# Two row tiles of x turned on TensorE, the rest by the crossbar, at the head of a linear-attention kernel

## The chip, the cores and the metric

The kernel runs on one core of one Trainium2 chip. The metric is the device time of one execution in microseconds (us). The profiled execution also has a span, from its first to its last instruction, which is about 1.7 us shorter than the time. All points in time in this text ("at 7.49 us") count from the start of that span. TensorE is PE in the profile, its weight loads PEld, VectorE DVE, ScalarE ACT, GpSimd POOL, SyncE SP. The crossbar is the DMA route that transposes a matrix while it loads it. A load lands when its last byte is there and the engines that wait for it are told. PSUM is the memory that TensorE writes to.

## The reference

```python
B, S, D = 1, 2048, 640                    # H = 32 heads of 20
qkv = (x @ wqkv) ...                      # q, k, v: [B, H, S, 20]
phi = lambda t: jnp.where(t > 0, t + 1, jnp.exp(t)) + 1e-6
pq, pk = phi(q), phi(k)
kv  = einsum("bhsd,bhse->bhde", pk, v);  z = einsum("bhsd->bhd", pk)
num = einsum("bhqd,bhde->bhqe", pq, kv); den = einsum("bhqd,bhd->bhq", pq, z)[..., None] + 1e-6
return (num / den) ... @ wo
```

The kernel never makes v. It makes phi(k) for all 16 row tiles of 128 rows first (the "K phase"), then P = x^T phi(k) (the "P phase"), and works on from there. The K phase needs x with the model dimension on the partitions (`xT`), the P phase needs x in its natural layout (`xn`).

## The kernel before

Each engine has its own list of instructions; a small planner adds a semaphore wait wherever one reads what another wrote.

```python
XCH = [(0, 256), (256, 512), (512, 1024), (1024, 1536), (1536, 2048)]
def load_xT():                                  # SP queue: crossbar transposes straight from HBM
    for i, (a, b) in enumerate(XCH):
        P.add("sp", lambda e, a=a, b=b: e.dma_start_transpose(
            xT[...][:, :, a:b], x[0, a:b, :]), writes=[("xT", i)], dma=True)

def load_wk():                                  # ACT queue: wk in two halves of its columns
    w_cols(wk, 0, HALF, D, ("wk", 0), "act")
    w_cols(wk, HALF, D, D, ("wk", 1), "act")
    ...                                         # (load of the ACT table)

def warm(n):                                    # fillers: matmuls of zeros that nobody reads
    for _ in range(n):
        P.add("pe", lambda e: e.matmul(bank(7), zero[:, 0:128], zero[:, :], start=True, stop=True), ...)

def k_tile(st):
    for h in range(2):                          # five matmuls 128x128 by 128x320 for each half of wk
        ...  P.add("pe", mm, reads=xT_keys(128 * st, 128 * st + 128) + [("wk", h)], ...)
    ...                                         # exp on ACT, two steps of phi on DVE

load_wk(); load_xT(); pool_const(); load_rest() # load_rest: wq, xn (natural x), wv, wo on the SP queue
permute_wq()
warm(16)
for st in range(NT):
    k_tile(st)
...                                             # P phase, q tiles, and the rest: untouched by the change
```

Of the kernel before, what the change touches and what calls it, by code (L numbers as in the profile page):

```python
# [7 lines left out]
ALU = mybir.AluOpType  # L8
BF16 = mybir.dt.bfloat16
# [73 lines left out]
def bass_standalone__linear_attn_block__prompt_kernel(nc, x, wqkv, wo, out):  # L83
    B, S, D = x.shape
    assert (B, S, D) == (1, 2048, 640)
    H, DH = 32, 20
    NC_ = D // 128
    NT = S // 128
    HALF = D // 2
# [5 lines left out]
    with contextlib.ExitStack() as ctx:  # L95
        es = ctx.enter_context

        def sb(name, cols, dt=BF16):
            return es(nc.sbuf_tensor(name, [128, cols], dt))

        xT = sb("xT", NC_ * S)
        xn = sb("xn", NT * D)
        wk = sb("wk", NC_ * D)
# [4 lines left out]
        pk = sb("pk", NT * D)  # L108
# [13 lines left out]
        ones = sb("ones", 8, F32)  # L122
        eps = sb("eps", 8, F32)
        zero = sb("zero", BK)
        lb = [sb(f"lb{j}", BK, F32) for j in range(2)]
        rd = [sb(f"rd{j}", BK) for j in range(2)]
        osb = [sb(f"osb{j}", D) for j in range(4)]
# [3 lines left out]
        P = Plan(nc, es)  # L131

        def bank(b, n=BK, off=0, parts=128):
            return ps[0:parts, BK * b + off:BK * b + off + n]

        def two_banks(b, n=HALF, parts=128):
            return ps[0:parts, BK * b:BK * b + 2 * BK].rearrange(
                "p (g j) -> p g j", j=BK)[:, :, 0:n]

        def fold(ap, j=HALF):  # L140
            return ap.rearrange("p (g j) -> p g j", j=j)


        def pool_const():
            P.add("dve", lambda e: e.memset(zero[:, :], 0.0), writes=["zero"])
            P.add("dve", lambda e: e.memset(ones[:, :], 1.0), writes=["ones"])
            P.add("dve", lambda e: e.memset(eps[:, :], 1e-6), writes=["eps"])  # L147
            P.add("pool", lambda e: e.memset(wv[:, NC_ * D:], 0.0), writes=["wvpad"])
            P.add("pool", lambda e: e.memset(hm[:, :], 1.0), writes=["hm"])
            P.add("pool", lambda e: e.memset(bm[:, :], 1.0), writes=["bm"])  # L150
            for t, w, name in ((hm, 4, "hm"), (bm, DH, "bm")):
                n = t.shape[1] // w
                for lo in (True, False):
                    P.add("pool", lambda e, t=t, w=w, n=n, lo=lo: e.affine_select(
                        out=t[:, :].rearrange("p (a b) -> p a b", b=w),
                        in_=t[:, :].rearrange("p (a b) -> p a b", b=w),
                        pattern=[[-w if lo else w, n], [0, w]],
                        base=0 if lo else w - 1,
                        channel_multiplier=1 if lo else -1,
                        compare_op=ALU.is_ge, fill=0.0), reads=[name], writes=[name])  # L160

        XCH = [(0, 256), (256, 512), (512, 1024), (1024, 1536), (1536, 2048)]

        def xch_of(row):
            return next(i for i, (a, b) in enumerate(XCH) if a <= row < b)

        def load_xT():
            for i, (a, b) in enumerate(XCH):
                P.add("sp", lambda e, a=a, b=b: e.dma_start_transpose(
                    xT[:, :].rearrange("p (c s) -> p c s", s=S)[:, :, a:b], x[0, a:b, :]),  # L170
                    writes=[("xT", i)], dma=True)

        def xT_keys(a, b):
            return [("xT", i) for i, (p, q) in enumerate(XCH) if p < b and a < q]

        def w_cols(dst, lo, hi, col, key, eng):
            P.add(eng, lambda e: e.dma_start(
                dst[:, 0:NC_ * D].rearrange("p (c n) -> p c n", n=D)[:, :, lo:hi],
                wqkv[:, col + lo:col + hi].rearrange("(c p) n -> p c n", p=128)),
                writes=[key], dma=True)  # L180

        def load_wk():
            w_cols(wk, 0, HALF, D, ("wk", 0), "act")
            w_cols(wk, HALF, D, D, ("wk", 1), "act")
            tl = mybir.InstLoadActFuncSet(
                name=nc.get_next_instruction_name(),
                act_func_set_id=ACT_TABLE_SET_LN_EXP, ins=[], outs=[])
            P.add("act", lambda e: e.add_instruction(tl), writes=["table"])

        def load_rest():  # L190
            w_cols(wqn, 0, D, 0, "wqn", "sp")
            for q in range(4):
                P.add("sp", lambda e, q=q: e.dma_start(
                    xn[:, 4 * q * D:4 * (q + 1) * D].rearrange("p (t n) -> p t n", n=D),
                    x[0, 512 * q:512 * (q + 1), :].rearrange("(t p) n -> p t n", p=128)),
                    writes=[("xn", q)], dma=True)
            w_cols(wv, 0, D, 2 * D, "wv", "sp")
            P.add("sp", lambda e: e.dma_start(
                wog[0:GW, 0:5 * D].rearrange("p (g n) -> p g n", n=D),
                wo[0:5 * GW, :].rearrange("(g p) n -> p g n", p=GW)),  # L200
                writes=["wog"], dma=True)
            P.add("sp", lambda e: e.dma_start(
                wog[0:gsz[5], 5 * D:6 * D], wo[5 * GW:D, :]), writes=["wog5"], dma=True)

        def permute_wq():

            for d in range(NC_):
                P.add("pool", lambda e, d=d: e.tensor_copy(  # L208
                    wqp[:, d * D:(d + 1) * D].rearrange("p (c h j) -> p c h j", c=NC_, j=4),
                    wqn[:, d * D:(d + 1) * D].rearrange("p (h c j) -> p c h j", c=NC_, j=4)),  # L210
                    reads=["wqn"], writes=[("wqp", d)])


        def warm(n):
            for _ in range(n):
                P.add("pe", lambda e: e.matmul(  # L216
                    bank(7), zero[:, 0:128], zero[:, :], start=True, stop=True),
                    reads=["zero"], writes=[("bank", 7)])

        def k_tile(st):  # L220
            b = 2 * (st % 4)
            for h in range(2):
                def mm(e, h=h):
                    for c in range(NC_):
                        r = e.matmul(  # L225
                            bank(b + h, HALF),
                            xT[:, c * S + 128 * st:c * S + 128 * st + 128],
                            wk[:, c * D + HALF * h:c * D + HALF * (h + 1)],
                            start=(c == 0), stop=(c == NC_ - 1))
                    return r  # L230
                P.add("pe", mm, reads=xT_keys(128 * st, 128 * st + 128) + [("wk", h)],
                      writes=[("bank", b + h)])
            banks = [("bank", b), ("bank", b + 1)]
            t = ek[st % 3]
            P.add("act", lambda e: e.activation(fold(t[:, :]), two_banks(b), ACTF.Exp),  # L235
                  reads=banks + ["table"], writes=[("ek", st % 3)])
            P.add("dve", lambda e: e.tensor_scalar(  # L237
                t[:, :], t[:, :], 1.0, 1e-6, ALU.min, ALU.add),
                reads=[("ek", st % 3)], writes=[("ek", st % 3)])
            P.add("dve", lambda e: e.scalar_tensor_tensor(  # L240
                fold(pk[:, st * D:(st + 1) * D]), two_banks(b), 0.0, fold(t[:, :]),
                ALU.max, ALU.add),
                reads=banks + [("ek", st % 3)], writes=[("pk", st)])

        def p_step(h, st):

            def mm(e):
                for d in range(NC_):
                    r = e.matmul(  # L249
                        bank(d, HALF), xn[:, st * D + 128 * d:st * D + 128 * d + 128],  # L250
                        pk[:, st * D + HALF * h:st * D + HALF * (h + 1)],
                        start=(st == 0), stop=(st == NT - 1))
                return r
            P.add("pe", mm, reads=[("xn", st // 4), ("pk", st)],
                  writes=[("bank", d) for d in range(NC_)])

        def p_out(h):
# [171 lines left out]
                reads=[("osb", j, 0), ("osb", j, 1)], writes=[("out", st)], dma=True)  # L429


        load_wk()
        load_xT()
        pool_const()
        load_rest()
        permute_wq()
        warm(16)
        for st in range(NT):
            k_tile(st)
        zst = z_steps()  # L440
        qs = [(s, c) for s in range(NSB) for c in range(NC_)]
        qi = [0]
# [5 lines left out]
        for h in range(2):  # L448
            for st in range(NT):
                p_step(h, st)  # L450
                if zst and st % 2 == 1:
                    zst.pop(0)()
                if st == 7:
                    next_q(5 + qi[0] % 3)
            p_out(h)
            next_q(5 + qi[0] % 3)
            next_q(5 + qi[0] % 3)
# [91 lines left out]
```

## Time and profile before

| | before |
|---|---|
| time, median of 4 runs (range) | 111.82 us (111.79 to 111.96) |
| span of the profiled run | 110.1 us |
| TensorE busy | 101.5 us, 92% |
| first K matmul | 7.49 us |
| first P matmul | 30.05 us |

The page's first part says that TensorE is the busy engine.

```profile
PE 101.5 (92%) x662; PEld 64.0 (58%) x668; DVE 66.9 (61%) x132; ACT 41.9 (38%) x73; POOL 5.9 (5%) x16
```

That figure counts 16 filler matmuls as work. What holds the start is in the chain of waits of the first 33 us (start us, length us, what). Each step was released by the one above it.

```profile
...
0.81 6.55 DMA xT<-in_x_dram
7.36 0.14 issue
7.49 20.55 PE ps L225 x150
...
30.05 3.02 PE ps L249 x21
```

The first crossbar transpose is issued at 0.81 us and takes 6.55 us to land. Then K (L225) runs, and then P (L249). TensorE's own list of waits says the same (who waited for whom: us in total, times, longest).

```profile
...
PE ps L225 <- DMA xT<-in_x_dram: 1.1, 1, 1.1
PE ps L249 <- DVE pk L240: 0.7, 1, 0.7
```

K has one wait, at its start. Behind it matmuls follow each other every 136 ns, 1.36 us for a row tile of ten, and K's 160 matmuls follow one another without a hole. P's wait of 0.7 us is for phi of a late K tile, and moves with K.

Landing times of each load, worked out from the trace as its issue plus its time to landing: wk's first half 4.71 us, its second half 7.35; crossbar pieces 7.36 (rows 0-255), 8.18 (256-511), 11.11 (512-1023), 14.47, 16.83.

### The profile page before, as it was taken

To read this page: it belongs to the slowest core of one execution; us is meant where nothing else is said; L and a number is where in the kernel's file an instruction comes from. 1 tells how busy PE (TensorE), PEld (TensorE's weight loads), DVE (VectorE), ACT (ScalarE), POOL (GpSimd) and SP (SyncE) were. 2 spreads that over 40 slices of the span, in tenths; PEclk is the share of its full clock that TensorE was granted. 3 is DMA by queue.
4 is the path that set the end of the run, shared out by engine and by line. 5 is a ranking of instruction groups with operands and counts; after the bars stand their busy time and mean duration, and the time that the engine had idled before them with its cause. 6 is when DMAs were issued, how large, how long until landed. Compare 5 with 4: busy or idle time off the path is not lost.

```text
span 110.1 us, 1693 instructions
## 1 busy us (share of the span) xinstructions
PE 101.5 (92%) x662; PEld 64.0 (58%) x668; DVE 66.9 (61%) x132; ACT 41.9 (38%) x73; POOL 5.9 (5%) x16
## 2 busy tenths in 40 slices
PE   5969999999799999999999999993999799999990
PEld 2327777777477674676757745431446377777760
DVE  1004888998899899701137664969849837333331
ACT  3104555555500206202043379872575173333330
POOL 7100000750000000000000000000000000000000
PEclk9999999999999999999999999999999999999999
DMA  1999999999980000000000000082720032433333
GB/s 40 270 295 220 224 211 298 378 363 364 258 163 22 0 0 3 0 0 0 6 0 3 0 0 0 18 216 70 206 92 0 0 119 92 152 119 119 119 120 118
DMA packets 19497, 12.88 MB, mean 117 GB/s; under 512 B 10914, under 2 KB 19490, under 8 KB 19490
## 3 DMA queue, kind: packets, MB, share of 16 engines
q1 hardware_dynamic: 18178, 11.96, 39.4%
q10 hardware_dynamic: 1312, 0.82, 2.7%
q8 instruction: 5, 0.08, 0.3%
q14 instruction: 2, 0.02, 0.0%
HBM read 6.72 MB, written 3.44 MB: 92 GB/s over the span
## 4 chain that ended last, share of the span: by engine, by line
PE 70%; DVE 15%; DMA 6%; ACT 5%; issue 1%
PE ps L225 19%; PE ps L416 17%; PE ps L249 15%; PE ps L275 12%; DMA xT<-in_x_dram 6%; DVE pq L288 4%; PE ps L391 4%; DVE za L294 4%; ACT eq L283 2%; DVE eq L285 2%; DVE pq L407 2%; PE ps L344 1%; ACT lb L398 1%; PE ps L365 1%; ACT rd L400 1%
## 5 line engine op out<-in xcount | busy, mean ns | idle before, releaser
L275 PE MATMUL ps<-xT,wqp 128*128 128x512 bf16 x95 | 23.0, 379 | 2.0 <-DVE pq L288 1.8
L249 PE MATMUL ps<-pk,xn 128*128 128x320 bf16 x160 | 22.4, 299 | 0.8 <-DVE pk L240 0.7
L225 PE MATMUL ps<-wk,xT 128*128 128x320 bf16 x160 | 21.9, 299 | 1.1 <-DMA xT<-in_x_dram 1.1
L416 PE MATMUL ps<-w2p,pq 128*128 128x320 bf16 x160 | 22.2, 299 | 0.3 <-DVE pq L288 0.3
L249 PEld LDWEIGHTS ps<-pk,xn 128*128 128x128 bf16 x160 | 15.5, 98 | 7.9 <-DVE pk L240 1.0
L225 PEld LDWEIGHTS ps<-wk,xT 128*128 128x128 bf16 x160 | 15.6, 98 | 7.5 <-issue 1.5
L283 ACT ACTIVATE eq<-ps 128x512 bf16<-128x512 f32 x20 | 11.9, 595 | 21.2 <-PE ps L275 20.7
L416 PEld LDWEIGHTS ps<-w2p,pq 128*128 128x128 bf16 x160 | 15.6, 98 | 7.0 <-DVE pq L288 0.6
L235 ACT ACTIVATE ek<-ps 128x640 bf16<-128x640 f32 x16 | 11.3, 704 | 15.7 <-PE ps L225 15.7
L275 PEld LDWEIGHTS ps<-xT,wqp 128*128 128x128 bf16 x100 | 9.6, 98 | 12.2 <-DVE pq L288 2.2
L288 DVE SCALAR_TENSOR_TENSOR pq<-ps,eq 128x512 bf16<-128x512 f32 x20 | 13.8, 692 | 0.7
L285 DVE TENSOR_SCALAR eq<-eq 128x512 bf16<-128x512 bf16 x20 | 5.8, 290 | 12.8 <-ACT eq L283 12.6
L240 DVE SCALAR_TENSOR_TENSOR pk<-ps,ek 128x640 bf16<-128x640 f32 x16 | 13.2, 824 | 0.6
L425 DVE CAST osb<-ps 128x320 bf16<-128x320 f32 x16 | 7.7, 489 | 9.6 <-PE ps L416 9.5
L237 DVE TENSOR_SCALAR ek<-ek 128x640 bf16<-128x640 bf16 x16 | 6.1, 380 | 10.5 <-ACT ek L235 10.4
L423 ACT CAST osb<-ps 128x320 bf16<-128x320 f32 x16 | 6.8, 425 | 12.6 <-PE ps L416 12.5
L407 DVE TENSOR_TENSOR pq<-pq,rd 128x512 bf16<-128x512 bf16 x20 | 7.0, 417 | 2.0 <-ACT rd L400 2.0
L216 PE MATMUL ps<-zero 128*128 128x512 bf16 x16 | 5.2, 494 | 1.3 <-DVE eps L147 1.3
L261 ACT CAST pt<-ps 128x320 bf16<-128x320 f32 x6 | 2.2, 434 | 9.7 <-PE ps L249 9.7
L294 DVE TENSOR_TENSOR za<-pk 128x1280 f32<-128x1280 bf16 x4 | 5.7, 1483 | 0.0
L391 PE MATMUL ps<-pq,zb 128*128 128x512 bf16 x19 | 4.8, 380 | 0.4 <-DVE pq L288 0.3
L208 POOL COPY wqp<-wqn 128x640 bf16<-128x640 bf16 x5 | 3.6, 756 | 16.9 <-DMA wqn<-in_wqkv_dram 16.9
(30 smaller groups left out, 36.1 us busy)
## 6 DMA issues: line engine op xcount, KB each, us to landing
xn<-in_x_dram SPq DMA_DIRECT2D x4, 640.0 KB, 9.7
out_dram<-osb SPq DMA_DIRECT2D x16, 160.0 KB, 1.8
wk<-in_wqkv_dram ACTq DMA_DIRECT2D x2, 400.0 KB, 5.0
wqn<-in_wqkv_dram SPq DMA_DIRECT2D x1, 800.0 KB, 5.2
wv<-in_wqkv_dram SPq DMA_DIRECT2D x1, 800.0 KB, 14.3
w2p<-w_rows SPq DMA_DIRECT2D x5, 160.0 KB, 2.7
wog<-in_wo_dram SPq DMA_DIRECT2D x1, 750.0 KB, 14.8
w_rows<-w2g SPq DMA_DIRECT2D x1, 750.0 KB, 5.3
```

What stands on the lines that cost most here:

```text
L225: r = e.matmul(bank(b + h, HALF), xT[:, c * S + 128 * st:c * S + 128 * st + 128], wk[:, c * D + HALF * h:c * D + HALF * (h + 1)], start=(c ...
L235: P.add("act", lambda e: e.activation(fold(t[:, :]), two_banks(b), ACTF.Exp), reads=banks + ["table"], writes=[("ek", st % 3)])
L240: P.add("dve", lambda e: e.scalar_tensor_tensor(fold(pk[:, st * D:(st + 1) * D]), two_banks(b), 0.0, fold(t[:, :]), ALU.max, ALU.add), rea ...
L249: r = e.matmul(bank(d, HALF), xn[:, st * D + 128 * d:st * D + 128 * d + 128], pk[:, st * D + HALF * h:st * D + HALF * (h + 1)], start=(st ...
L275: r = e.matmul(bank(b), wqp[:, d * D + 128 * c:d * D + 128 * c + 128], xT[:, d * S + BK * sbk:d * S + BK * (sbk + 1)], start=(d == 0), sto ...
L283: P.add("act", lambda e: e.activation(t[:, :], bank(b), ACTF.Exp), reads=[("bank", b), "table"], writes=[("eq", i)])
L285: P.add("dve", lambda e: e.tensor_scalar(t[:, :], t[:, :], 1.0, 1e-6, ALU.min, ALU.add), reads=[("eq", i)], writes=[("eq", i)])
L288: P.add("dve", lambda e: e.scalar_tensor_tensor(pq[:, c * S + BK * sbk:c * S + BK * (sbk + 1)], bank(b), 0.0, t[:, :], ALU.max, ALU.add), ...
L294: P.add("dve", lambda e: e.tensor_tensor(d_ap, a, b, ALU.add), reads=ra + rb, writes=[dst])
L391: r = e.matmul(bank(b), zb[:, 128 * c:128 * c + 128], pq[:, c * S + BK * sbk:c * S + BK * (sbk + 1)], start=(c == 0), stop=(c == NC_ - 1))
L407: P.add("dve", lambda e, v=v: e.tensor_tensor(v, v, rd[i][:, :], ALU.mult), reads=[("rd", i), ("pq", sbk, c)], writes=[("pq", sbk, c)])
L416: r = e.matmul(bank(b + h, HALF), pq[:, c * S + 128 * st:c * S + 128 * st + 128], w2p[:, c * D + HALF * h:c * D + HALF * (h + 1)], start=( ...
```

## The change

The intent is to get the first rows of x sooner. Row tiles 0 and 1 are loaded in natural layout by plain DMAs, first of all on the ACT queue; TensorE turns them (ten transposes of 128x128 through an identity matrix), and DVE copies them out of PSUM into `xT`. They are bytes that the P phase loads anyway. The crossbar starts at row 256, and only after x tile 0 has landed. Seven of the 16 fillers go. The first two K tiles are done half by half, so that both use wk's first half before the second is wanted.

```diff
+            P.add("pool", lambda e: e.memset(ident[:, :], 0.0), writes=["ident"])
+            P.add("pool", lambda e: e.affine_select(out=ident[:, :], ..., fill=1.0), ...)
...
-        XCH = [(0, 256), (256, 512), (512, 1024), (1024, 1536), (1536, 2048)]
+        NPE = 2
+        XCH = [(0, 128), (128, 256), (256, 512), (512, 1024), (1024, 1536), (1536, 2048)]
...
-            for i, (a, b) in enumerate(XCH):
+            for i, (a, b) in enumerate(XCH[NPE:]):
                 P.add("sp", lambda e, a=a, b=b: e.dma_start_transpose(...),
-                    writes=[("xT", i)], dma=True)
+                    reads=[("xn", 0)] if i == 0 else [],
+                    writes=[("xT", NPE + i)], dma=True)
+        def transpose_x(st, b):
+            v = bank(b, HALF).bitcast(BF16)
+            def mm(e):
+                for c in range(NC_):
+                    r = e.transpose(v[:, 128 * c:128 * c + 128],
+                                    xn[:, st * D + 128 * c:st * D + 128 * c + 128], ident[:, :])
+                return r
+            P.add("pe", mm, reads=[("xn", st), "ident"], writes=[("bank", b)])
+            P.add("dve", lambda e: e.tensor_copy(xT[...][:, :, 128 * st:128 * st + 128], v...), ...)
...
         def load_wk():
+            for t in range(NPE):
+                load_xn(t, t + 1, "act")
             w_cols(wk, 0, HALF, D, ("wk", 0), "act")
             w_cols(wk, HALF, D, D, ("wk", 1), "act")
...
-        warm(16)
-        for st in range(NT):
-            k_tile(st)
+        warm(5)
+        for st in range(NPE):
+            transpose_x(st, 6 + st)
+        warm(4)
+        for h in range(2):
+            for st in range(NPE):
+                k_half(st, h)
+        for st in range(NPE):
+            k_phi(st)
+        for st in range(NPE, NT):
+            k_half(st, 0)
+            k_half(st, 1)
+            k_phi(st)
```

(k_tile is split into k_half and k_phi, fillers write bank 4 and not 7, the later loads of xn start at tile 2, the P phase waits for xn tile by tile, and pool_const, which makes the identity matrix, is called first.)

More of the change, by code (lines that the diff above doesn't have):

```diff
@@ L124, in bass_standalone__linear_attn_block__prompt_kernel @@
         zero = sb("zero", BK)
+        ident = sb("ident", 128)
         lb = [sb(f"lb{j}", BK, F32) for j in range(2)]
@@ L147, in pool_const @@
             P.add("dve", lambda e: e.memset(eps[:, :], 1e-6), writes=["eps"])
+            P.add("pool", lambda e: e.memset(ident[:, :], 0.0), writes=["ident"])
+            P.add("pool", lambda e: e.affine_select(
+                out=ident[:, :], in_=ident[:, :], pattern=[[-1, 128]], base=0,
+                channel_multiplier=1, compare_op=ALU.not_equal, fill=1.0),
+                reads=["ident"], writes=["ident"])
             P.add("pool", lambda e: e.memset(wv[:, NC_ * D:], 0.0), writes=["wvpad"])
@@ L167, in load_xT @@
         def load_xT():
-            for i, (a, b) in enumerate(XCH):
+            for i, (a, b) in enumerate(XCH[NPE:]):
                 P.add("sp", lambda e, a=a, b=b: e.dma_start_transpose(
                     xT[:, :].rearrange("p (c s) -> p c s", s=S)[:, :, a:b], x[0, a:b, :]),
-                    writes=[("xT", i)], dma=True)
+                    reads=[("xn", 0)] if i == 0 else [],
[8 more added lines that the diff above has]
+            P.add("pe", mm, reads=[("xn", st), "ident"], writes=[("bank", b)])
+            P.add("dve", lambda e: e.tensor_copy(
+                xT[:, :].rearrange("p (c s) -> p c s", s=S)[:, :, 128 * st:128 * st + 128],
+                v.rearrange("p (c s) -> p c s", s=128)),
+                reads=[("bank", b)], writes=[("xT", st)])
         def xT_keys(a, b):
@@ L180, in w_cols, with load_xn @@
                 writes=[key], dma=True)
+        def load_xn(a, b, eng):
+            P.add(eng, lambda e: e.dma_start(
+                xn[:, a * D:b * D].rearrange("p (t n) -> p t n", n=D),
+                x[0, 128 * a:128 * b, :].rearrange("(t p) n -> p t n", p=128)),
+                writes=[("xn", t) for t in range(a, b)], dma=True)
         def load_wk():
+            for t in range(NPE):
+                load_xn(t, t + 1, "act")
             w_cols(wk, 0, HALF, D, ("wk", 0), "act")
@@ L191, in load_rest @@
             w_cols(wqn, 0, D, 0, "wqn", "sp")
-            for q in range(4):
-                P.add("sp", lambda e, q=q: e.dma_start(
-                    xn[:, 4 * q * D:4 * (q + 1) * D].rearrange("p (t n) -> p t n", n=D),
-                    x[0, 512 * q:512 * (q + 1), :].rearrange("(t p) n -> p t n", p=128)),
-                    writes=[("xn", q)], dma=True)
+            for a, b in ((NPE, 4), (4, 8), (8, 12), (12, 16)):
+                load_xn(a, b, "sp")
             w_cols(wv, 0, D, 2 * D, "wv", "sp")
@@ L216, in warm, with k_half, mm, k_phi @@
                 P.add("pe", lambda e: e.matmul(
-                    bank(7), zero[:, 0:128], zero[:, :], start=True, stop=True),
-                    reads=["zero"], writes=[("bank", 7)])
-        def k_tile(st):
+                    bank(4), zero[:, 0:128], zero[:, :], start=True, stop=True),
+                    reads=["zero"], writes=[("bank", 4)])
+        def k_half(st, h):
             b = 2 * (st % 4)
-            for h in range(2):
-                def mm(e, h=h):
-                    for c in range(NC_):
-                        r = e.matmul(
-                            bank(b + h, HALF),
-                            xT[:, c * S + 128 * st:c * S + 128 * st + 128],
-                            wk[:, c * D + HALF * h:c * D + HALF * (h + 1)],
-                            start=(c == 0), stop=(c == NC_ - 1))
-                    return r
-                P.add("pe", mm, reads=xT_keys(128 * st, 128 * st + 128) + [("wk", h)],
-                      writes=[("bank", b + h)])
+            def mm(e):
+                for c in range(NC_):
+                    r = e.matmul(
+                        bank(b + h, HALF),
+                        xT[:, c * S + 128 * st:c * S + 128 * st + 128],
+                        wk[:, c * D + HALF * h:c * D + HALF * (h + 1)],
+                        start=(c == 0), stop=(c == NC_ - 1))
+                return r
+            P.add("pe", mm, reads=xT_keys(128 * st, 128 * st + 128) + [("wk", h)],
+                  writes=[("bank", b + h)])
+        def k_phi(st):
+            b = 2 * (st % 4)
             banks = [("bank", b), ("bank", b + 1)]
@@ L253, in mm @@
                 return r
-            P.add("pe", mm, reads=[("xn", st // 4), ("pk", st)],
+            P.add("pe", mm, reads=[("xn", st), ("pk", st)],
                   writes=[("bank", d) for d in range(NC_)])
@@ L429, in out_tile @@
                 reads=[("osb", j, 0), ("osb", j, 1)], writes=[("out", st)], dma=True)
+        pool_const()
         load_wk()
         load_xT()
-        pool_const()
         load_rest()
         permute_wq()
-        warm(16)
-        for st in range(NT):
-            k_tile(st)
+        warm(5)
[11 more added lines that the diff above has]
+            k_phi(st)
         zst = z_steps()
```

## The prediction

> **What bounds the kernel now.** TensorE: busy 101.5 of 110.1 us (92%, the page's first part), and the chain of waits is 70% TensorE. The change touches only the head. There TensorE waits 1.08 us (the list of waits: K projection on the crossbar transpose of x), after 16 filler matmuls that compute nothing. The K projection starts at 7.49 us: the first crossbar transpose (rows 0-255), issued at 0.81, landed at 7.36, and the second half of wk at 7.35. From there K runs without a gap, 136 ns from matmul to matmul, 1.36 us per row tile, to about 29.3; the next phase starts at 30.05. Everything after hangs on the end of K, not on a load (wv lands at 33, wo at 35, used near 57). So the change is worth what it moves the end of K, at most.
>
> **What changes.** Removed: one crossbar transpose of 256 rows (1280 packets of 256 B, about 2 us of the DMA engines while wk wants them). Added: 10 TensorE transposes, two VectorE copies of 128x640 out of PSUM, one select on GpSimd (about 0.56 us, as hm's). The two x tiles are not extra bytes; they are loaded later anyway. Seven filler matmuls go. Moved: xn tiles 0 and 1 stand ahead of wk on the ACT queue, and all crossbar transposes wait until xn tile 0 has landed.
>
> **New schedule (estimates from the trace).** Stores of the same 128x640 shape take 1.8 us from issue to landing, and wk's first packets came 1.1 us after issue with a slow ramp, so xn 0 lands at about 3.1, xn 1 at 3.5. Five fillers at the cold pitch of 427 ns end at 3.4. Transposes 3.4-4.6, each copy 0.5-0.8 us (a 128x320 fp32 copy takes 0.49), xT ready at about 5.5. wk at the 290 GB/s it reached alone: first half lands at about 5.3, second at about 7.0 (before 4.71 and 7.35). K starts at about 5.7; the order of halves (both tiles on half 0, then both on half 1) hides the second half. Tiles 0 and 1 end at about 8.5, against 10.2 before.
>
> Then the crossbar decides. Its transposes took 5.3 to 6.6 us from issue to landing; issued at 3.2, rows 256-511 land at about 8.6 (before 8.18) and rows 512-1023, 2.9 us later as before, at about 11.5-11.9 (before 11.11). Row tile 4 started at 12.93 before; it can start at about 11.7 now. Later chunks come every 3.3 us for four tiles that take 5.4, so they do not bind. xn and wq land within 1 us of before, early enough.
>
> **On the critical path:** about 1.2 us gained of the possible 1.7; the rest is lost to the delayed crossbar stream. No copy or transpose costs path time.
>
> **Clock.** The Trainium skill, "TensorE: Matmul & The Clock Gate" (Part 1; Part 4), says that the clock opens after about 3.4 us of sustained work and that transposes do not count as such. Here it opened at 4.4 us (pitch 427 to 216 ns), 3.15 us after the first filler. With five fillers, then transposes, it may open later, up to about 7.8; then K begins at half speed and the gain falls to about 0.7.
>
> **Prediction:** 110.6 us, 110.1 to 111.3 in 8 of 10. Faster by over 2%: 0.04; within 2%: 0.94; slower by over 2%: 0.02.
>
> **Right if:** K starts at 5.4-6.2; a wait of K on the crossbar of 0.1-1 us stands at row tile 2 or 4; K ends 0.7-1.6 us earlier; everything later is the same, shifted. **Wrong if:** the first xn lands after 4 us; a cold clock lasts into K's later tiles; the crossbar stream runs over 1 us later than I say (gain near 0); or it runs sooner, with wk out of its way (gain 1.7 or more).

## More of the kernel before

The loads fight for the DMA engines. In the stretch from 4 to 5 us the queue table of before reads as follows (q1 is the SP queue with the crossbar transposes, q10 the ACT queue with wk; packets, MB, time as a share of the 16 engines).

```profile
q1 hardware_dynamic: 987, 0.25, 116.8%
q10 hardware_dynamic: 60, 0.03, 10.8%
```

wk gets 0.03 MB in that microsecond, the crossbar 0.25.

## The result, and the profile after

| | before | after |
|---|---|---|
| time, median of 4 runs each (range) | 111.82 us (111.79 to 111.96) | 110.75 us (110.53 to 110.94) |
| ratio, 95% interval | | 0.9901 (0.9877 to 0.9926) |
| span of the profiled run | 110.1 us | 108.8 us |
| first K matmul | 7.49 us | 6.13 us |
| first P matmul | 30.05 us | 28.69 us |

A ratio is the mean time of one kernel's fast runs over the mean of the other's fast runs of the same rounds, so it is not quite the ratio of the medians. The change is 1.0% faster, inside the 2% that count as the same.

The labels fast and slow need a word for what follows. On one core a run is called slow when it is over 1.5% above the fastest run of the same kernel. Some experiments below have a wide spread of their own, and then the label falls on a part of that spread.

The page's line of busy times and the chain of waits of the first 33 us, after:

```profile
PE 101.2 (93%) x665; PEld 64.4 (59%) x671; DVE 67.3 (62%) x134; ACT 41.9 (38%) x73; POOL 6.4 (6%) x18
```

```profile
...
1.26 2.31 PE ps L244 x5
3.57 1.07 PE ps L187 x10
4.64 1.65 PE ps L244 x4
6.29 20.39 PE ps L253 x150
...
28.69 4.38 PE ps L280 x31
```

The crossbar has left the chain. From 1.26 us on TensorE itself is the chain: five fillers (L244), ten transposes (L187), four fillers, K (L253), P (L280). (The chain counts a piece from the modelled end of the one before it, so K stands at 6.29 us though its first matmul starts at 6.13.) Its whole list of waits has no line for K any more:

```profile
PE ps L306 <- DVE pq L319: 1.8, 1, 1.8
PE ps L244 <- DVE eps L148: 1.3, 1, 1.3
PE ps L280 <- DVE pk L271: 0.7, 1, 0.7
PE ps L447 <- DVE pq L319: 0.3, 1, 0.3
PE ps L422 <- DVE pq L319: 0.3, 1, 0.3
```

In the stretch from 4 to 5 us wk now has the DMA engines for itself, since the crossbar was held back:

```profile
q10 hardware_dynamic: 493, 0.31, 114.8%
```

Landings after, from the trace: x tile 0 at 3.05 us, x tile 1 at 3.66, wk's halves at 5.93 and 7.12, crossbar pieces at 8.38 (rows 256-511), 11.41 (512-1023), 14.46, 18.31. K wants the two early crossbar pieces at 8.85 and 11.57 us (6.13 plus two and four times 1.36), so they are in time, the second by 0.16 us.

**The gain of K's start reaches the end.** From 7.49 to 6.13 is 1.36 us; from 30.05 to 28.69 is 1.36; from the span's 110.14 to 108.79 is 1.35. In all fourteen traces, whatever the kernel, the time from the first P matmul to the end of the span lies between 80.09 and 80.12 us. Every difference between the traced runs arises before P.

### The profile page after: what moved, and what is told of

The parts are those of the page before. It is cut to its first block, busy times and chain, and to the rows that moved or that the text cites. A ratio compares the mean times of both kernels' runs of the same rounds, so it can differ in the third digit from the quotient of the medians.

```text
span 108.8 us, 1705 instructions
## 1 busy us (share of the span) xinstructions
PE 101.2 (93%) x665; PEld 64.4 (59%) x671; DVE 67.3 (62%) x134; ACT 41.9 (38%) x73; POOL 6.4 (6%) x18
## 4 chain that ended last, share of the span: by engine, by line
PE 75%; DVE 16%; ACT 5%; issue 1%
PE ps L253 19%; PE ps L447 17%; PE ps L280 15%; PE ps L306 12%; DVE pq L319 4%; PE ps L422 4%; DVE za L325 4%; PE ps L244 4%; ACT eq L314 2%; DVE eq L316 2%; DVE pq L438 2%; PE ps L375 1%; ACT lb L429 1%; PE ps L396 1%; PE ps L187 1%
## 5 line engine op out<-in xcount | busy, mean ns | idle before, releaser
L280 PE MATMUL ps<-pk,xn 128*128 128x320 bf16 x160 | 22.4, 299 | 0.8 <-DVE pk L271 0.7
L253 PE MATMUL ps<-wk,xT 128*128 128x320 bf16 x160 | 21.9, 299 | 0.0
L280 PEld LDWEIGHTS ps<-pk,xn 128*128 128x128 bf16 x160 | 15.5, 98 | 7.9 <-DVE pk L271 1.0
L314 ACT ACTIVATE eq<-ps 128x512 bf16<-128x512 f32 x20 | 11.9, 594 | 21.2 <-PE ps L306 20.7
L253 PEld LDWEIGHTS ps<-wk,xT 128*128 128x128 bf16 x160 | 15.7, 98 | 6.6 <-DMA wk<-in_wqkv_dram 0.5
L266 ACT ACTIVATE ek<-ps 128x640 bf16<-128x640 f32 x16 | 11.2, 704 | 13.5 <-PE ps L253 13.5
L268 DVE TENSOR_SCALAR ek<-ek 128x640 bf16<-128x640 bf16 x16 | 5.4, 338 | 5.8 <-ACT ek L266 5.7
L244 PE MATMUL ps<-zero 128*128 128x512 bf16 x9 | 4.2, 625 | 1.3 <-DVE eps L148 1.3
```

Source lines behind the costliest of these rows:

```text
L244: P.add("pe", lambda e: e.matmul(bank(4), zero[:, 0:128], zero[:, :], start=True, stop=True), reads=["zero"], writes=[("bank", 4)])
L253: r = e.matmul(bank(b + h, HALF), xT[:, c * S + 128 * st:c * S + 128 * st + 128], wk[:, c * D + HALF * h:c * D + HALF * (h + 1)], start=(c ...
L266: P.add("act", lambda e: e.activation(fold(t[:, :]), two_banks(b), ACTF.Exp), reads=banks + ["table"], writes=[("ek", st % 3)])
L280: r = e.matmul(bank(d, HALF), xn[:, st * D + 128 * d:st * D + 128 * d + 128], pk[:, st * D + HALF * h:st * D + HALF * (h + 1)], start=(st ...
L314: P.add("act", lambda e: e.activation(t[:, :], bank(b), ACTF.Exp), reads=[("bank", b), "table"], writes=[("eq", i)])
```

## The experiments

Theory: K's start is held by three arrivals that lie close together, wk's first half, the x tiles, and TensorE's own fillers on a slow clock. Rivals: the crossbar stream, delayed by the change, is the true bound (the prediction's view); a smaller first crossbar piece would have given the same gain; the gate on the crossbar is only a loss. There were twelve runs of kernels, all correct; one of them, e10_again, is the change itself. They ran in groups on different chips, and each ratio is to runs of the kernel before on the same chip. A matmul on the slow clock is called cold.

### e1_order: the old order of the first two K tiles

```diff
-        for h in range(2):
-            for st in range(NPE):
+        for st in range(NPE):
+            for h in range(2):
                 k_half(st, h)
```

> The changed kernel with the first two K tiles in the old order (tile 0 on both halves of wk, then tile 1) and nothing else changed. In the trace of the change, K starts at 6.13 us, the second half of wk lands at 7.12, and with the old order it would be wanted at 6.81. Theory (the load of wk paces the head, and the order of halves hides part of it): a wait of about 0.3 to 0.4 us on wk inside K, and 0.3 us more in all (about 0.3% slower than the change). Rival (the crossbar, which had only 0.16 us to spare at row tile 4, sets the end of K): the time is the same to 0.15 us.

Measured: 111.00 us (110.82 to 111.32), ratio to before 0.9921 (0.9907 to 0.9935). A line of TensorE's list of waits, and the chain in the head:

```profile
PE ps L253 <- DMA wk<-in_wqkv_dram: 0.6, 1, 0.6
```

```profile
...
2.20 5.16 DMA wk<-in_wqkv_dram
7.36 0.05 issue
7.41 1.67 PE ps L253 x11
```

K stops after its first five matmuls and waits for wk's second half, which landed at 7.36 us. The first P matmul came at 29.29 us, 0.60 later than in the trace of the change. So the wait is shown, and with it that wk paces the head in this order. Its price in the timed runs is not resolved: the interval overlaps the change's. The rival (crossbar) had no wait in this trace.

### e2_nogate: the crossbar does not wait for x tile 0

```diff
-                    reads=[("xn", 0)] if i == 0 else [],
+                    reads=[],
```

> The changed kernel without the wait of the crossbar transposes for the first x tile; they are issued at 0.8 us again. Theory (the head is paced by what reaches wk, so keeping the crossbar off the DMA engines is part of the gain): wk's first half lands later than 5.93, at about 6.5 to 7, K starts that much later, and the time rises by 0.4 to 0.9 us against the change. Rival (the gate is only a loss, the crossbar is the bound): the crossbar's chunks land about 2 us earlier and the time falls by 0.1 us or more.

Measured: 115.21, 115.54, 117.86, 118.56, 118.62, 118.84 us. The two fast runs give a ratio of 1.0308 (1.0289 to 1.0327): at least 3% slower than before. This was the largest effect, and the theory had its size wrong (0.4 to 0.9 us expected against the change, about 4.5 us measured in the fast runs, over 7 in the slow). The profiled run is slow (118.56 us). Its waits, the clock row of its page (tenths of full speed in 40 slices), and the time to landing of wk's two halves:

```profile
PE ps L253 <- DMA wk<-in_wqkv_dram: 3.0, 1, 3.0
...
PE ps L187 <- DMA xn<-in_x_dram: 1.3, 1, 1.3
```

```profile
PEclk9999558999999999999999999999999999999999
```

```profile
DMA to landing us min/median/max: 5.3/7.9/10.4
```

wk's second half took 10.4 us and landed at 12.56; the second crossbar piece was in flight for the same 10.5 us, from 2.22 to 12.75. x tile 1 landed at 5.50 and not 3.66. TensorE stood idle for 3 us, and in this run its clock, once open at 8.38 us, fell back to half for 6.83 us (the two slices that read 5 and the one that reads 8). P came 8.05 us later in this trace than in the change. The sum comes out of it: K began 1.63 us later, the wait for wk's second half took about 3.2 us from K's flow, and the K matmuls at the pitch of 267 ns another 3.2. So starts and waits cost about 4.8 us and the clock the rest. The fast runs, at a mean granted clock of 0.997 and 1.000, are over 4 us behind the change, which fits the first part alone. But they were not traced, and the mean leaves out the time before the clock first opens, so their split is not shown. With this layout of loads, holding the crossbar back is a necessary part of the change, not a price of it.

### e3_nofill2 and e5_nofill: fewer fillers, and none

```diff
# e3_nofill2                # e5_nofill
-        warm(4)            -        warm(5)
                            -        warm(4)
```

> The changed kernel without the four filler matmuls after the transposes. In the trace of the change the fillers end at 6.13 us and the first half of wk has landed at 5.93, and the clock opened at 6.11, 1.7 us after the transposes. Theory (fillers keep the clock's activity up; transposes alone do not open it): K starts at about 6.0, but on the half clock (267 ns pitch instead of 136) for 1 us or more, so the time is 0.4 to 1.2 us longer than the change. Rival (the clock opens anyway, the fillers only occupy the engine): 0.1 to 0.2 us shorter.

> The changed kernel without any filler matmul: TensorE does nothing before the ten transposes. If transposes count for the clock like matmuls, or if K's own matmuls open it at once, K starts at about 6.0 us and loses 0.5 us or less, time 111.2 or less. If only sustained matmuls open it, K runs on the half clock for the rest of one 3.4 us stretch and perhaps a whole one, 2 to 6 us in all, and loses half of that: time 1 to 3 us above the change, 111.8 to 113.8 us.

Measured, e3_nofill2: two runs at 110.70 and 110.87 us, four at 112.05, 112.12, 112.39 and 112.47. The label slow cuts through the late group (the last two have it), so the ratio of the four runs called fast, 1.0005 (0.9965 to 1.0044), mixes both groups. The profiled one is the fastest. Measured, e5_nofill: 112.06, 112.51, 112.97, 113.15 us; ratio to before 1.0052 (1.0017 to 1.0087). TensorE's timeline in the two traces (start us, length us, ..., idle time before it):

```profile
...
6.01 7.23 PE L253 MATMUL ps<-wk,xT 128*128 128x320 bf16 x50 [1.37 <-DMA wk<-in_wqkv_dram]
```

```profile
...
5.86 7.33 PE L253 MATMUL ps<-wk,xT 128*128 128x320 bf16 x33 [1.48 <-DMA wk<-in_wqkv_dram]
```

Both start K within 0.3 us of the change. In the same 7.2 to 7.3 us the first did 50 K matmuls, the second 33. The stretches of the second (e5_nofill) show where: TensorE's matmuls stand in the first brackets.

```profile
6.00:8.00 2.00, 2.00 (x9) 1.09 (x8) 0.00 (x0) 0.00 (x0) 0.00 (x0) 1.00 1.28 267
8.00:10.00 2.00, 2.00 (x9) 1.18 (x8) 0.00 (x0) 0.00 (x0) 0.00 (x0) 1.00 1.19 267
...
12.00:14.00 2.00, 2.00 (x17) 1.43 (x16) 1.56 (x5) 0.82 (x2) 0.00 (x0) 1.00 0.90 198
```

The counts take in matmuls that overlap an edge: nine in 2 us belong to the pitch of 267 ns, 17 to the pitch of 136. 21 K matmuls ran at the slow pitch, about 130 ns too long each, which is 2.7 us. K had begun 0.27 us earlier than in the change, and P started 2.42 us later: the sum comes out. (The clock column reads 1.00 here because this trace has no record of the clock; the pitch tells.) So the fillers are not idle ornament: the five in front alone leave four of six runs 1.2 to 1.8 us later than the other two, about half of one 3.4 us stretch, and none leaves every run late. That the four late runs of e3_nofill2 have cold K matmuls is an inference; no trace caught one.

This is where the clock comes in. The Trainium skill, "TensorE: Matmul & The Clock Gate", Part 1, says that the gate looks at free-running windows of 3413 ns and that the moment of opening therefore differs from run to run. The traces agree: from opening to closing the change's clock record lasts 102.40 us, 30 windows, and before's 105.81, 31 windows, while they opened at 6.11 and 4.40 us.

### e4_before128 and e11_b128fill12: only a smaller first crossbar piece

```diff
# both, on the kernel before                           # e11_b128fill12 also
-        XCH = [(0, 256), (256, 512), ...              -        warm(16)
+        XCH = [(0, 128), (128, 256), (256, 512), ...  +        warm(12)
```

> The kernel before with its first crossbar transpose cut into two of 128 rows; nothing moves to TensorE. If the gain came only from a smaller first piece, K would start earlier here too: about 6.5 us instead of 7.49, and the time would fall by up to 1 us. If the crossbar's time from issue to landing hardly depends on the rows[...], K starts at 7.0 to 7.4 and the time is within 0.4 us of before.

> The kernel before with the first crossbar transpose cut into two of 128 rows and 12 fillers, not 16; nothing on TensorE. With 16 fillers K started at 7.20 us at the fillers' end, though the crossbar's first piece had landed at 6.93. If the crossbar's time to landing is the floor of that route, K starts at 6.9 to 7.1 and the time is 111.2 to 111.5 us, short of the change by 0.5 us or more. If it reaches the change's 110.75 within 0.2 us, TensorE's transposes were not needed for the gain.

Measured, e4_before128: 111.48 us (111.40 to 112.07), ratio 0.9968 (0.9951 to 0.9985). Measured, e11_b128fill12: 111.52 us (111.18 to 111.85), ratio 0.9956 (0.9936 to 0.9976). Their chains, e4_before128 first:

```profile
...
1.26 6.10 PE ps L216 x16
7.36 1.77 PE ps L225 x13
```

```profile
...
0.81 5.89 DMA xT<-in_x_dram
6.70 0.05 issue
6.74 2.35 PE ps L225 x16
```

With 128 rows the first piece took 6.12 and 5.89 us to land, against 6.55 for 256 rows. Half the rows bring 0.4 to 0.7 us. In e4_before128 the fillers, twelve of them slow in that run, ended after it and became the bound; with 12 the crossbar is the bound again. With the loads in their old order this is good for 0.3% to 0.4% of time, less than half of the change's 1.0%. On the chip of e11_b128fill12 the change itself (e10_again, below) ran at 0.9909 (0.9892 to 0.9926), and the two intervals do not meet. A plain load of one x tile took 2.25 us from issue to landing in the change. That is the difference in arrival, but not all of it has to be the crossbar's own. In the change the x tiles stand ahead of wk; in these two kernels the first crossbar pieces share the DMA engines with wk (in e11_b128fill12 wk's second half landed at 6.32 us and the two pieces of 128 rows at 6.70 and 6.91). No run put a crossbar piece ahead of wk, so how much of the gain needs TensorE, and how much is only the order of the loads, is not shown.

### e6_gate1: the crossbar waits for x tile 1

```diff
-                    reads=[("xn", 0)] if i == 0 else [],
+                    reads=[("xn", 1)] if i == 0 else [],
```

> The changed kernel with the crossbar waiting for x tile 1 (3.6 us) and not for tile 0 (3.05 us). In the trace of the change the second crossbar chunk landed at 11.41 us, 0.16 us before row tile 4 wanted it. If the crossbar is the next bound that close, it now lands near 12.0 and K waits 0.3 to 0.5 us at row tile 4: 0.2 to 0.45 us slower than the change. If the later issue is made up because wk is out of the way sooner (wk's second half lands before 7.0), no wait: the same to 0.15 us.

Measured: 110.18, 110.37, 110.59, 111.15, 111.16, 111.43 us; ratio 0.9895 (0.9862 to 0.9927), the change's own. The crossbar was issued at 3.58 us, 0.52 later than in the change, and its first two pieces landed at 8.51 and 11.54, only 0.13 later. K had no wait on it. Neither branch of the expectation describes this: the later issue was made up although wk's second half was not sooner (7.30). In this trace the crossbar's arrival followed the traffic ahead of it more than its own issue. The margin at row tile 4 was 0.02 us in this trace, so a wait there in the slower runs is possible; none was traced.

### e7_wkrows: wk in blocks of whole rows

```diff
-            w_cols(wk, 0, HALF, D, ("wk", 0), "act")
-            w_cols(wk, HALF, D, D, ("wk", 1), "act")
+            for j, (c0, c1) in enumerate([(0, 3), (3, 5)]):     # rows 128*c0 to 128*c1, all columns
+                ...  wk[:, c0 * D:c1 * D] <- wqkv[128 * c0:128 * c1, D:2 * D]
-        warm(4)
+        warm(2)
# tiles 0 and 1: both halves of both tiles on block 0, then on block 1
```

> The changed kernel with wk loaded as two blocks of whole rows (1280-byte packets, which moved at up to 384 GB/s in the trace of before, against 290 for the 640-byte packets of the halves), K of the first two tiles ordered by these blocks, and two fillers after the transposes and not four. wk's first block should land at about 5.2 us and the second at about 6.2 (5.93 and 7.12 in the change). K starts at about 5.3. If the crossbar then binds, tile 2 or 4 waits 0.3 to 0.8 us in all and the gain over the change is 0.1 to 0.4 us; if it does not bind, 0.7 us or more.

Measured: 110.86, 111.06, 111.41, 111.54, 112.53, 112.79 us; ratio of the four fast runs 0.9931 (0.9907 to 0.9954). That is no gain on the change (the intervals overlap, so a loss is not resolved either), and two runs came at over 112.5 us. The first block, a fifth larger than a half, landed at 6.37 us, the second at 7.32. The idea that larger packets would bring wk sooner fell: all of wk came no sooner than in halves (7.00 to 7.59 in the traces with halves on one queue and the gate). K started at 6.41 behind an idle gap of 0.92 us, and with two fillers the spread grew.

### e8_four: four x tiles on TensorE

```diff
-        NPE = 2
+        NPE = 4            # x tiles 2 and 3 on the ACT queue behind wk; crossbar from row 512, after x tile 1
# wk in row blocks and warm(2) as in e7_wkrows; tiles 2 and 3 are turned between the first K tiles
```

> As the kernel with row blocks of wk, and four x tiles, not two, in natural layout and turned by TensorE; the crossbar starts at row 512 and waits for x tile 1. The extra ten transposes cost about 0.6 us of TensorE at full clock (56 ns each), but no row tile should wait on the crossbar. If wk's load and TensorE alone bound the head, K ends 0.2 to 0.5 us earlier than in the change (time about 110.2 to 110.5). If the extra x loads or copies stall the first tiles, it is the same or slower.

Measured: 111.33, 112.01, 113.26, 113.65, 113.81, 113.96 us; the two fast runs give 0.9971 (0.9939 to 1.0003). Slower than the change, by intervals that do not meet. In the profiled run (111.33) K started at 6.36 us and its last matmul began 22.17 us later, against 21.60 in the change: the ten extra transposes cost 0.57 us of TensorE, as expected, and bought nothing, because no K tile was waiting for the crossbar. Before K it stood idle for 1.58 us. Three of the slow runs have a mean granted clock of 0.985; over 112 us that is 3.4 us at half speed, one more window (worked out, not traced).

### e9_twoq: wk's first half on the other queue

```diff
-            w_cols(wk, 0, HALF, D, ("wk", 0), "act")
+            w_cols(wk, 0, HALF, D, ("wk", 0), "sp")       # ahead of the crossbar
# crossbar after x tile 1; its piece 512-1023 cut in two; warm(3) after the transposes
```

> The changed kernel with the first half of wk issued on the SP queue at 0.8 us, beside the x tiles on the ACT queue, and not behind them; the crossbar waits for x tile 1, its 512-row chunk at row 512 is cut in two of 256, and three fillers stand after the transposes and not four (they end at 5.7 us on the cold clock). Theory (wk's arrival is what holds K): wk's first half lands at 5.3 to 5.6 us against 5.9 to 6.1, K starts at 5.7, and K ends 0.2 to 0.4 us earlier, so 110.2 to 110.5 us where the change has about 110.75. If x tile 1 is what suffers (lands after 4.3 us), the transposes and K start no earlier and nothing is gained.

Measured: 112.98 us (112.22 to 113.29), ratio 1.0072 (1.0041 to 1.0102): 0.7% slower than before. The chain:

```profile
...
1.25 3.75 DMA xn<-in_x_dram
5.00 0.04 issue
5.04 0.71 PE ps L187 x5
5.75 1.28 PE ps L244 x3
7.03 2.13 PE ps L253 x8
```

wk's first half landed at 4.55 us, sooner than hoped, and all of wk by 6.23. But x tile 1 now shared the engines with it and landed at 5.00, not 3.66. Its transposes, three slow fillers and the half clock stood between that and K, which began at 6.83 and ran 15 matmuls slowly (14 pitches of 267 ns; the clock opened at 10.67). The second branch of the expectation held: what counts is the last of the arrivals, and the order of TensorE's work must follow the arrivals.

### e10_again: the change once more

> The changed kernel, unaltered, once more, for its spread and a second trace. If the spread of 0.4 us seen (110.53 to 110.94) is the phase of the clock's stretches, the fillers and the first K matmuls differ: where the clock opens before 5.5 us K starts at wk's landing (5.9 to 6.1), where it opens after 6.2 us some K matmuls run at the 267 ns pitch, each costing 0.13 us, up to 0.5 us in all. If the spread is the DMA engines' alone, no K matmul is cold and wk's landing or a crossbar wait moves instead. Median 110.5 to 111.0.

Measured: 110.76, 110.93, 111.03, 111.04, 111.10 us; ratio 0.9909 (0.9892 to 0.9926). The result of the change is confirmed on another chip. Its chain in the head:

```profile
...
1.72 4.58 DMA wk<-in_wqkv_dram
6.30 0.05 issue
6.35 2.75 PE ps L253 x19
```

Here the clock opened at 4.30 us, so the fillers were over early, and K waited 0.94 us for wk's first half, which landed at 6.30 (5.93 in the other trace). In the first trace the fillers on the slow clock ended 0.2 us after wk had landed. So both bounds are real and nearly equal, and which of them ends last depends on the run. No K matmul was cold in either trace. What makes the spread between runs is not settled: wk's arrival moved by 0.5 us between the traces with the change's own load order, and the clock's window moves too.

### e12_early: a version put together from the runs

```diff
-            w_cols(wk, 0, HALF, D, ("wk", 0), "act")
+            w_cols(wk, 0, HALF, D, ("wk", 0), "sp")
-        XCH = [..., (256, 512), (512, 1024), ...
+        XCH = [..., (256, 512), (512, 768), (768, 1024), ...
-        for st in range(NPE): transpose_x(st, 6 + st)
-        warm(4)
-        (both tiles on half 0, then both on half 1, then phi of both)
+        transpose_x(0, 6)
+        warm(2)
+        k_half(0, 0)
+        transpose_x(1, 7)
+        k_half(0, 1); k_phi(0)        # then tiles 1 to 15 in order
```

> A version put together from the runs. wk's first half goes on the SP queue at 0.8 us (in the run with two queues it landed at 4.55 us and all of wk by 6.23, against 5.9 and 7.1 to 7.6 in the change), the crossbar waits for x tile 0 as in the change and its 512-row chunk at row 512 is cut in two. TensorE does x tile 0's transposes, two fillers, K of tile 0 on half 0, only then x tile 1's transposes (that tile landed at 5.0 us in the two-queue run), then the rest. K starts at 4.7 to 5.0 us. Theory (wk's and x's arrival and the clock pace the head): on an open clock row tile 2 starts at 8.0 to 8.6 us (8.85 in the change), on a late clock at about 9.0; time 110.0 to 110.7 us, a gain of 0.1 to 0.9 us on the change. If the crossbar, issued at about 3.4 us, is the bound after all, a wait on it of 0.3 us or more shows at row tile 2, and the time is no better than the change.

Measured: 110.18 us (110.08 to 110.78), ratio to before 0.9857 (0.9830 to 0.9883). It beats before by 1.4% and the change by about 0.5% (0.9857 against 0.9901 and 0.9909; its interval lies below that of e10_again, and just meets that of the first measurement). TensorE's part of the timeline:

```profile
...
4.78 0.88 PE L253 MATMUL ps<-wk,xT 128*128 128x320 bf16 x5
...
5.50 0.44 PE L187 MATMUL ps<-ident,xn 128*128 128x128 bf16 x5
...
6.33 4.93 PE L253 MATMUL ps<-wk,xT 128*128 128x320 bf16 x35 [0.39 <-DMA wk<-in_wqkv_dram]
```

K's first five matmuls run at 4.78 us, before x tile 1 is even there, in the place of fillers. wk's second half then landed at 6.29 us (7.12 and 7.47 in the change) and is the only wait left in K, 0.39 us. The crossbar pieces landed at 7.54, 9.32 and 11.33 and were wanted at 8.37, 11.09 and 13.81 (6.33 plus 15 matmuls, then two and four tiles more), so none bound. Why wk came sooner, in the stretches of TensorE and DMA (last column GB/s), e10_again first, then e12_early:

```profile
3.00:4.00 1.00, 1.00 (x8) 1.00 0.74 161
4.00:5.00 1.00, 1.00 (x9) 1.00 1.01 305
```

```profile
3.00:4.00 1.00, 1.00 (x8) 1.00 1.10 341
4.00:5.00 1.00, 1.00 (x6) 1.00 1.10 368
```

With everything on one queue the DMA engines fall to 161 GB/s between the x tiles and wk (233 in the other trace of the change); with wk beside them on the second queue they do not. From 2 to 6 us, adding up the four microseconds, e12_early moved 1.22 MB and the change 1.07 (e10_again) and 1.11 (first trace), although e12_early was the slower of them from 2 to 3 us (181 GB/s against 271 and 268). The other trace with two queues agrees: from 2 to 5 us e9_twoq and e12_early moved 0.89 MB each, and the six traces with wk's halves on one queue and the gate 0.66 to 0.81. The rest of the difference lies at wk's end. After 6 us the change still had 80 and 110 of wk's 1280 packets to move, and they ran among the crossbar's first packets until 6.71 and 7.06; e12_early had none left. The version changes the queue, the order of TensorE's work, the number of fillers and a crossbar piece at once; which of them brings the gain on the change is argued from the trace, not tested one by one.

## Why the prediction was right, point by point

The time came out where the prediction put it (110.6 predicted, 110.75 measured, range 110.1 to 111.3), and the gain was of the size predicted: 1.2 us against 1.07 of the medians and 1.36 in the traces. But one of its steps was wrong and one of its terms was off, and the sum was right partly by luck, because the two errors cancelled. Of its own conditions for being right, one failed: no wait of K on the crossbar of 0.1 to 1 us stood at row tile 2 or 4.

- **Right: only the head matters, and K's end carries all of it.** 80.09 to 80.12 us from P to the end in every trace.
- **Right: the arrivals of x and the first part of TensorE's schedule.** x tiles at 3.05 and 3.66 us (3.1 and 3.5 predicted), fillers to 3.37 (3.4), transposes 3.37 to 4.43 (3.4 to 4.6), copies of 0.49 us (0.5 to 0.8). A 640-column bf16 copy out of PSUM took as long (492 ns) as a 320-column copy from fp32 in PSUM (489). The Trainium skill, "VectorE: DVE Perf Modes", "Why PSUM operands drop a tier", gives a 16-bit operand in PSUM up to twice the rate of fp32, and this agrees.
- **Wrong term: "K starts at about 5.7".** It was 6.13 in one trace and 6.35 in the other. The prediction had wk's first half at 5.3; it landed at 5.93 and 6.30. It took 290 GB/s for the ACT queue alone. That holds between 4 and 6 us (307), but the prediction did not see the dip between 3 and 4 us. And the sum left out the four fillers after the transposes, which end at 6.13 on the slow clock.
- **Wrong step: "Then the crossbar decides."** No K tile waited for it in either trace of the change, nor with the gate moved half a microsecond later (e6_gate1). Its landings were predicted well (8.38 and 11.41 us, where 8.6 and 11.5-11.9 were written), but since K started later than predicted, they were in time. "The rest is lost to the delayed crossbar stream" is therefore false: the rest was lost before K's first matmul. Row tile 4 was predicted at about 11.7 us and came at 11.57, but as K's 41st matmul in an unbroken row, not as the end of a wait. The margin is thin (0.16, 0.06 and 0.02 us at row tile 4 in the traces of the change, of e10_again and of e6_gate1), so a K started much sooner with that layout would meet it; the two smaller pieces of e12_early moved it out of the way.
- **Right: wk's second half hides behind the new order.** Without it K waits 0.56 us (e1_order). It hid in both traces of the change, but not in every run of that order: in e3_nofill2 wk's second half landed at 7.59 us and K lost about 0.25 us to it.
- **The clock, given as a danger:** it did not strike the change in the traces. It is real, though: with fewer fillers most runs are about 1 us or more late (e3_nofill2, e5_nofill), and the trace of e5_nofill shows the cold matmuls. Not settled is whether transposes count for it. The Trainium skill, "TensorE: Matmul & The Clock Gate", Part 4, says that they do not count as busy in the same way. In e3_nofill2 the window that ended with the opening at 4.57 us held 2.1 us of fillers (62% of 3.41) and 1.1 us of transposes; in e5_nofill the window that ended at about 7.9 us (one window before the opening at 11.2 to 11.4) held 1.9 to 2.1 us of slow K matmuls (56 to 62%) and did not open. That leans to transposes counting, but the two shares touch each other, and two windows are not a proof.
- **"No copy or transpose costs path time" was too simple.** In the first trace fillers and transposes are the chain, 0.2 us behind wk's landing; with wk as the bound (e10_again) they are free.

## What to carry to other kernels

At the head of a kernel, list what the first useful matmul needs, and issue exactly that first; hold back a bulk stream that is needed later until the first loads are through, because here letting it start early cost over 4 us. For the first tile, a plain load ahead of wk landed about 4 us sooner than the crossbar's first piece beside wk, and was turned and copied 1.6 us later, while for the later tiles the crossbar was in time and free of TensorE work. Put real work in the place of fillers as soon as its data is there, in the order in which the data lands, and keep TensorE dense until its clock has opened.

## What the Trainium skill lacked or had wrong

- "Advanced Engine Details and Errata", "X-Bar Transpose (TRN2)", calls transposing DMAs as fast as regular ones and expects 350 to 400 GB/s. The rate of a long stream was 290 GB/s here, near the 307 of wk's plain 640-byte packets, but the latency is not alike: 5.9 to 6.1 us from issue to landing for the first 128 rows of x, 6.55 for 256, against 2.25 for a plain load of 128 rows. These crossbar pieces had wk beside them and the plain load stood in front of it, so the two figures are not for the same traffic; with the crossbar held back, pieces of 256 rows took 4.3 to 5.8. The page has no latency for it.
- "DMA: Bandwidth & Descriptors", "Rules for kernel authors", says that spreading DMAs over the issuing engines does not help bandwidth. Here, with the crossbar held back the same way, wk's first half moved to the second queue brought all of wk by 6.29 us and not by 7.12 to 7.47, with 341 GB/s and not 161 to 233 from 3 to 4 us, in which the one queue passes from one load to the next (0.89 MB and not 0.66 to 0.81 from 2 to 5 us). The order of landing changes with it (x tile 1 at 5.0 to 5.1 us and not 3.66).
- No page says how badly a crossbar stream can hold up a plain load beside it: wk's second half took 10.4 us in e2_nogate and 4.9 in the change, with the crossbar held back.
- "TensorE: Matmul & The Clock Gate", Part 1: the window of 3413 ns and its free run are confirmed (30 and 31 whole windows). Part 4, on transposes not counting for the clock: two windows here lean against it (above), unsettled. The same part's 275 to 390 ns for a transpose of 128x128 is the length of one (314 ns here, by the profile's modelled ends); back to back on the slow clock they follow each other every 107 ns, and every 56 ns once the clock is open (e8_four, e12_early).
